# One PSUM tile for each bank in place of four tiles of two banks, in a kernel of attention and two expert layers

## The chip, the cores and the metric

The kernel runs on one core of one Trainium2 chip. The metric is device time in microseconds (us): three runs of the kernel before took 1152.51, 1151.09 and 1156.83 us, with a median of 1152.51 us. Lower is better.

## The reference

Four sequences with eight heads of 576 positions and 64 features go through a causal attention with a decay, and the 2304 rows that come out of it go through two layers of 512 by 2048 by 512.

```python
def _attn_ref(q, k, v, f):
    scores = scale * np.matmul(q, k.transpose(0, 1, 3, 2))
    log_f = np.log(np.clip(f, 0.0001, 1.0))
    cum = np.cumsum(log_f, axis=-1)
    decay = cum[:, :, :, None] - cum[:, :, None, :]
    scores = np.where(causal, -1000000000.0, scores + decay)
    scores = scores - np.max(scores, axis=-1, keepdims=True)
    attn = np.exp(scores)
    attn = attn / (np.sum(attn, axis=-1, keepdims=True) + 1e-09)
    return np.matmul(attn, v)

def _moe_ref(x, w_in, w_out, alpha):
    h = x @ w_in
    g = np.maximum(h, 0.0) + alpha * np.minimum(h, 0.0)
    return g @ w_out

def _moe2_ref(x, w_in, w_out):
    h = x @ w_in
    sp = np.where(h > 20.0, h, np.log1p(np.exp(np.minimum(h, 20.0))))
    return (h * np.tanh(sp)) @ w_out
```

## The kernel before, in words

**Attention** (`stage_T`, `stage_M`, `stage_S`, `stage_R`, `stage_V`) handles two heads at a time, 16 pairs in all. `stage_M` finds the row maxima from a first product of queries and keys (L610, L612), which VectorE reduces (L620). `stage_S` computes the scores in four pieces, 288 columns of each head in two of them and 512 in the other two (L658), and ScalarE takes the exponential of both heads of a piece in one instruction (L666). GpSimd masks the diagonal blocks (L674) and adds up (L689). `stage_R` sums over the keys with a product with ones (L701), takes the reciprocal by a logarithm and an exponential on ScalarE (L706, L707) and refines it on VectorE (L708, L710). `stage_V` multiplies by the values (L731) and writes the result to X (L737).

**The layers** work on six blocks of 384 rows. Each operand is split in a high and a low part, so that a product takes three matmuls: L775, L776 and L777 for the first matrix, L840, L841 and L842 for the second one of layer one, L851, L852 and L853 for the second one of layer two. The first four of the sixteen column groups of layer one are done apart (`group_a`), the first three blocks of that while attention still runs. `prelu` (L794, L796, L800, L803) and `mish` (L820 to L832) lie between the two matrices. `mish` takes the exponential e of h on ScalarE (L820), works on it with VectorE and ScalarE, writes an intermediate u into PSUM bank 3 (L826) and reads it back (L828). L830 reads h once more and L832 multiplies on GpSimd; the split for the second matrix is L322 on ScalarE and L332 on VectorE.

**PSUM** has eight banks of 512 columns. They are allocated as four tiles of two banks, and the names of single banks are views of these tiles:

```python
banks2 = [psum.tile([P, 2, 512], F32, tag=f"b{n}", name=f"b{n}") for n in range(4)]
banks = {n: banks2[n // 2][:, n % 2] for n in range(8)}
```

In attention the pairs 0-1, 2-3 and 4-5 are handed out as wholes, one bank for each head. Bank 6 belongs to `stage_V` and bank 7 to `group_a`. In the layers banks 4 to 7 take h in turn (`bH`), and banks 0 to 3 hold the sums of the second matrix (`bA`). Layer two has only three sums (banks 0, 1 and 2, each 128 rows by 512 columns); u is in bank 3.

**What sets the order.** Every operation is put in a plan with its engine, an estimated cost, the keys that it reads and writes, and a due time. `Plan.emit` makes a list schedule of them, ten passes long, and issues the instructions in the order of the best pass. The keys name single banks. The waits themselves are set afterwards by the tile layer from the tiles that an instruction touches, in the order of issue. An engine works on its instructions in that order.

Of the kernel before, what the change touches and what calls it, by code (L numbers as in the profile page):

```python
# [237 lines left out]
def fox_attention__then__moe_prelu__then__moe_mish(  # L238
# [52 lines left out]
    psum = pool("psum", space=PSUM)  # L291
    banks2 = [psum.tile([P, 2, 512], F32, tag=f"b{n}", name=f"b{n}") for n in range(4)]
    banks = {n: banks2[n // 2][:, n % 2] for n in range(8)}

# [170 lines left out]
    SK = NQ * P  # L465
    plan.share("two", banks2[:3])
    plan.share("one", [banks[6]])
# [51 lines left out]
    def prologue():  # L519

        V, G = nc.vector, nc.gpsimd
        pk = [("P", 1, s) for s in range(len(PIECES))]
        plan.stage("pro2")
# [37 lines left out]
    def load_bias(pr, at):  # L561
        plan.stage("LB2")
        i = pr % 2
        for e in range(2):
            h = 2 * pr + e
            src = (lambda h=h: bias[h:h + 1]) if pr == 0 else (lambda h=h: biasd[h:h + 1])
            dma(at, lambda e=e, src=src: nc.sync.dma_start(BK[i][e * HALF:e * HALF + 3, :S].bitcast(F32), src().rearrange("h t n -> (h t) n") if pr else src()),
                7, r=(["bh", "bl", "bias1"] + [("P", 1, s) for s in range(len(PIECES))] if pr == 0 else ["biasd"]) + [("BK", i)],
                w=[("BKr", i, e)], issue=0.62)
# [21 lines left out]
    def stage_M(pr, at):  # L591
# [4 lines left out]
        for c in [NQ - 1, 0] + list(range(NQ - 2, 0, -1)):  # L596
# [5 lines left out]
            for n, (a, z) in enumerate(pieces):  # L602
# [25 lines left out]
        def tr():  # L628
            for c in range(NQ):
                q0 = rows(c)[0]  # L630
                half = int(q0 >= W0)
                nc.tensor.transpose(ps()[:, half, q0 - half * W0:q0 - half * W0 + P], M5[i][:, c], ident)
        plan.add("PE", 0.11 * NQ, at + 6, tr, ["ident"] + [("M5", i, c) for c in range(NQ)], [bk, ("BQ", i, 0), ("BQ", i, 1)], mode="t")
        for half, (a, z) in enumerate(((0, W0), (W0, S))):
            def fn(e, half=half, a=a, z=z):
                if e == "ACT":
                    nc.scalar.activation(BQ[i][:, a:z], ps()[:, half, :z - a], AF.Identity, bias=bvec)
                else:
                    nc.vector.tensor_scalar(BQ[i][:, a:z], ps()[:, half, :z - a], bvec, None, op0=ALU.add)
            plan.add({"ACT": c_act(z - a, True, 1), "DVE": c_dve(z - a)}, 0.0, at + 6.5, fn, [bk, "bvec"], [("BQ", i, half)])  # L640

    def stage_S(pr, at):

        i = pr % 2
        for s, piece in enumerate(PIECES):
# [4 lines left out]
            def mm(ps=ps, piece=piece):  # L650
                x = 0
                for j, a, z in piece:
# [3 lines left out]
                    for m, (l_, r_) in enumerate(passes):  # L656
                        for e in range(2):
                            nc.tensor.matmul(ps()[:, e, x:x + z - a], l_[hs[e]], r_[hs[e]], start=m == 0, stop=m == len(passes) - 1)  # L658
                    x += z - a
                if pr == 0:  # L660
# [3 lines left out]
                     [(x, i, j) for x in ("hi", "lo") for j in range(2)] + [("BQ", i, x) for x in halves]  # L664
                     + [("BKr", i, e) for e in range(2)] + [("BK", i), ("kpad", i)], [bk, ("P", i, s)], mode="k")
# [15 lines left out]
    def stage_R(pr, at):  # L681
# [8 lines left out]
        for n, j in enumerate((1, 4, 2, 3)):  # L690
            w = 2 * (S - j * P)
            plan.add({"POOL": c_pool(w, 2.25), "DVE": c_dve(w)}, 0.0, at + 0.8 * n, lambda e, j=j, w=w: add(j, e, w),
                     [("P", i, 2 if j in (1, 4) else 3)] + [("P", i, 0), ("P", i, 1)] * (j == 1), ["acc"], port=BOTH)
        ps, bk = plan.use("two")
        h2 = S // 2

        def mm():
            for half, a, z in ((0, 0, P), (0, P, h2), (1, h2, S)):
                for e in range(2):
                    src = pt_at(i, e, 0, a, z) if z == P else acc_t[:, e, a - P:z - P]  # L700
                    nc.tensor.matmul(ps()[hs[e], half, a - half * h2:z - half * h2], ones, src, start=True, stop=True)  # L701
        plan.add("PE", 4 * S / 2.4e3 + 0.02, at + 4, mm, ["acc", "ones", ("P", i, 0)], [bk, "rr", "uu"], mode="c")
        sv = lambda: ps()[:, :, :h2]
        v2 = lambda t: t.rearrange("p (a n) -> p a n", a=2)
# [5 lines left out]
        plan.add("DVE", c_dve(S), at + 6, lambda: V.scalar_tensor_tensor(  # L710
            out=uu, in0=uu, scalar=2.0, in1=rr, op0=ALU.subtract, op1=ALU.mult), ["uu", "rr"], ["uu"], port=BOTH)

    def stage_V(pr, at):
# [3 lines left out]
        for n, (a0, z) in enumerate(WIN):  # L717
# [15 lines left out]
            rk = [("P", i, s) for s, p in enumerate(PIECES) if any(y > a0 and x < z for _, x, y in p)]  # L733
            plan.add("PE", 4 * sum((y - x) / 2.4 + 2 for _, x, y in mm) / 1e3, at + n, run,
# [296 lines left out]
```

## Time and profile before

| | |
|---|---|
| median of three runs | 1152.51 us |
| profiled execution | 1155.68 us, of which the span is 1154.0 us |
| mean granted TensorE clock | 0.975 of full speed |
| TensorE matmuls, busy | 1062.2 us, 6332 instructions |
| TensorE weight loads, busy | 922.8 us |
| VectorE, ScalarE, GpSimd, busy | 775.4, 513.8 and 421.4 us |

In the profile PE is TensorE with its matmuls and PEld its weight loads, one for each matmul of the layers; both are counted busy for themselves, since a load overlaps the matmul ahead of it. DVE is VectorE, ACT ScalarE, POOL GpSimd. Attention takes the first 310 us, and the first three blocks of `group_a` are woven into it. Then come the other three blocks of `group_a` (to some 450 us), the rest of layer one with the conversion of the weights of layer two beside it (to some 693 us, where the first exponential of `mish` starts), and layer two.

### The profile page before, as it was taken

The page shows a single profiled execution, that of the slowest core. Times are in us where ns is not written, and L with a number is a line of the kernel's source. Part 1 is how long each engine was busy: PE and PEld are TensorE (multiplying, and loading weights), DVE is VectorE, ACT ScalarE, POOL GpSimd, SP SyncE. Part 2 cuts the span into 40 slices and gives each one's busy share as a digit, 9 for nine tenths or more (in the row PEclk, how much of TensorE's full clock was granted, in tenths as well). Part 3 has the DMA queues.
Part 4 walks back from the last instruction along what each step waited for, and adds up shares of the span by engine and source line. Part 5 has one row for each costly group of instructions (what it writes and reads, how often), then busy time and mean ns, then how long its engine had stood idle before and what let it go on. Part 6 is the DMA issues. An engine that isn't in the chain of part 4 may idle for free.

```text
span 1154.0 us, 17414 instructions
## 1 busy us (share of the span) xinstructions
PE 1062.2 (92%) x6332; PEld 922.8 (80%) x6332; DVE 775.4 (67%) x1670; ACT 513.8 (45%) x1021; POOL 421.4 (37%) x416
## 2 busy tenths in 40 slices
PE   7899899898979989999999999989989989999998
PEld 6666677776768889899999998768777778778896
DVE  7677866755376776778621368678867777786785
ACT  3455444444345543434332355444444444454443
POOL 2554554544345462323233242232232322323222
PEclk9878999999989999999999999999999999999999
DMA  5232212100033344545500133000000000000000
GB/s 173 79 92 84 79 35 63 53 23 22 19 119 101 110 128 154 181 153 189 164 1 1 46 110 92 10 0 28 1 10 19 1 28 1 1 28 1 28 1 28
DMA packets 55207, 70.86 MB, mean 61 GB/s; under 512 B 6576, under 2 KB 32176, under 8 KB 55120
## 3 DMA queue, kind: packets, MB, share of 16 engines
q1 hardware_dynamic: 55120, 69.75, 19.5%
q8 instruction: 49, 0.80, 0.3%
q14 instruction: 38, 0.31, 0.1%
HBM read 56.39 MB, written 13.33 MB: 60 GB/s over the span
## 4 chain that ended last, share of the span: by engine, by line
PE 69%; DVE 16%; ACT 5%; issue 5%; DMA 3%; POOL 1%; SPq 1%; DVEq 0%; POOLq 0%; ACTq 0%
PE b L775 11%; PE b L777 9%; PE b L776 9%; PE b L851 6%; PE b L853 5%; PE b L852 5%; PE b L840 5%; PE b L658 4%; PE b L842 4%; PE b L841 4%; PE b L731 4%; DVE b L826 3%; DVE junk L620 2%; DVE x L828 1%; DMA raw<-in_moe_w_in_dram 1%
## 5 line engine op out<-in xcount | busy, mean ns | idle before, releaser
L775 PE MATMUL b<-xh,w 128*128 128x384 f32 x768 | 269.6, 351 | 42.3 <-DVE x L830 10.4
L777 PE MATMUL b<-xl,w 128*128 128x384 f32 x768 | 260.2, 339 | 1.0 <-DVE xl L332 1.0
L776 PE MATMUL b<-xh,w 128*128 128x384 f32 x768 | 259.8, 338 | 0.0
L832 POOL TENSOR_TENSOR x<-x 128x384 f32<-128x384 f32 x96 | 112.8, 1175 | 310.3 <-DVE x L830 192.8
L775 PEld LDWEIGHTS b<-xh,w 128*128 128x128 f32 x768 | 145.9, 190 | 72.9 <-DVE x L830 14.5
L776 PEld LDWEIGHTS b<-xh,w 128*128 128x128 f32 x768 | 146.2, 190 | 3.2
L777 PEld LDWEIGHTS b<-xl,w 128*128 128x128 f32 x768 | 145.9, 190 | 1.5 <-DVE xl L332 1.5
L322 ACT CAST g<-x 128x384 fp32r<-128x384 f32 x120 | 61.4, 512 | 181.6 <-POOL x L832 157.0
L840 PE MATMUL b<-g,w 128*128 128x384 f32 x384 | 134.2, 349 | 8.2 <-DVE x L803 4.2
L332 POOL TENSOR_TENSOR g<-X,g 128x384 fp32r<-128x384 f32 x72 | 77.7, 1083 | 165.2 <-ACT g L322 118.1
L842 PE MATMUL b<-g,w 128*128 128x384 f32 x384 | 130.7, 340 | 0.6 <-DVE g L332 0.6
L851 PE MATMUL b<-w,g 128*128 128x512 f32 x288 | 117.1, 407 | 15.1 <-DVE b L826 10.2
L841 PE MATMUL b<-g,w 128*128 128x384 f32 x384 | 130.6, 340 | 0.0
L853 PE MATMUL b<-w,g 128*128 128x512 f32 x288 | 113.5, 394 | 0.7 <-DVE g L332 0.7
L852 PE MATMUL b<-w,g 128*128 128x512 f32 x288 | 113.3, 394 | 0.0
L800 DVE SCALAR_TENSOR_TENSOR X<-X,alph,b 128x384 f32<-128x384 f32 x72 | 43.7, 611 | 84.1 <-ACT X L794 74.0
L826 DVE SCALAR_TENSOR_TENSOR b<-x 128x384 f32<-128x384 f32 x96 | 66.9, 697 | 46.1 <-PE b L853 36.5
L620 DVE CUSTOM_DVE_ANT_0 junk<-b,tri 128x320 f32<-128x320 f32 (+3 forms) x160 | 69.2, 433 | 26.6 <-PE b L612 19.0
L840 PEld LDWEIGHTS b<-g,w 128*128 128x128 f32 x384 | 73.8, 192 | 15.5 <-DVE x L803 5.5
L851 PEld LDWEIGHTS b<-w,g 128*128 128x128 f32 x288 | 54.0, 188 | 37.6 <-DVE b L826 21.4
L794 ACT ACTIVATE X<-b 128x384 f32<-128x384 f32 x72 | 34.9, 490 | 104.1 <-PE b L777 89.9
L332 POOL TENSOR_TENSOR w<-wb,w 128x512 fp32r<-128x512 f32 x32 | 47.5, 1485 | 91.6 <-ACT w L322 91.6
(94 smaller groups left out, 2010.8 us busy)
## 6 DMA issues: line engine op xcount, KB each, us to landing
raw<-in_moe_w_in_dram SPq DMA_DIRECT2D x64, 256.0 KB
raw<-in_moe_w_out_dram SPq DMA_DIRECT2D x64, 256.0 KB
wd<-wb SPq DMA_DIRECT2D x32, 256.0 KB
raw<-wd SPq DMA_DIRECT2D x32, 256.0 KB
qkr<-in_q_dram SPq DMA_DIRECT2D x16, 288.0 KB
qkr<-in_k_dram SPq DMA_DIRECT2D x16, 288.0 KB
out_dram<-x SPq DMA_DIRECT2D x18, 256.0 KB
vt<-in_v_dram SPq DMA_DIRECT2D x16, 256.0 KB
```

The lines of the kernel that those rows point to most:

```text
L332: plan.add(engs, 0.0, at, lambda e: (nc.gpsimd if e == "POOL" else nc.vector).tensor_tensor(out=out(), in0=in0(), in1=in1(), op=ALU.subtra ...
L775: nc.tensor.matmul(ps[:, :NB], w[:, 0, c], xh[c], start=(c == 0), stop=False)
L776: nc.tensor.matmul(ps[:, :NB], w[:, 1, c], xh[c], start=False, stop=False)
L777: nc.tensor.matmul(ps[:, :NB], w[:, 0, c], xl[c], start=False, stop=(c == KC - 1))
L826: add("DVE", c_dve(NB), lambda e, m: V.scalar_tensor_tensor(out=u, in0=m, scalar=2.0, in1=e, op0=ALU.add, op1=ALU.mult), [mk, ek], [uk], BOTH)
L832: add("POOL", c_pool(NB, 2.2), lambda e, m: nc.gpsimd.tensor_tensor(out=m, in0=e, in1=m, op=ALU.mult), [ek, mk], [mk])
L840: nc.tensor.matmul(ps[:, :NB], w[:, 0, c], g[:, 0], start=first, stop=False)
L841: nc.tensor.matmul(ps[:, :NB], w[:, 1, c], g[:, 0], start=False, stop=False)
L842: nc.tensor.matmul(ps[:, :NB], w[:, 0, c], g[:, 1], start=False, stop=last)
L851: nc.tensor.matmul(ps, g[:, 0, sl], w[:, 0], start=first, stop=False)
L852: nc.tensor.matmul(ps, g[:, 0, sl], w[:, 1], start=False, stop=False)
L853: nc.tensor.matmul(ps, g[:, 1, sl], w[:, 0], start=False, stop=last)
```

## The change

Each of the eight banks becomes a tile. The pairs of attention are pairs of tiles. An instruction cannot read two tiles as one operand, so what read both banks of a pair at once becomes two instructions: the 64 exponentials of `stage_S` become 128, the 16 logarithms of `stage_R` 32, and the 16 products of the sum with its reciprocal (L708) 32. The keys of the probabilities become one for each head. The layers' code is the same but for the tiles that it writes into. The core of the diff (left out: the same change of index or key in the prologue, in the bias loads, in the transposes of `stage_M` and in `stage_V`):

```diff
-    banks2 = [psum.tile([P, 2, 512], F32, tag=f"b{n}", name=f"b{n}") for n in range(4)]
-    banks = {n: banks2[n // 2][:, n % 2] for n in range(8)}
+    banks = {n: psum.tile([P, 512], F32, tag=f"b{n}", name=f"b{n}") for n in range(8)}
...
-    plan.share("two", banks2[:3])
+    plan.share("two", [(banks[2 * n], banks[2 * n + 1]) for n in range(3)])
...
-                            nc.tensor.matmul(ps()[:, e, x:x + z - a], l_[hs[e]], r_[hs[e]], start=m == 0, stop=m == len(passes) - 1)
+                            nc.tensor.matmul(ps()[e][:, x:x + z - a], l_[hs[e]], r_[hs[e]], start=m == 0, stop=m == len(passes) - 1)
...
-            plan.add("ACT", c_act(2 * pw[s]), ai, lambda ps=ps, s=s: nc.scalar.activation(
-                Pt[i][:, :, poff[s]:poff[s] + pw[s]], ps()[:, :, :pw[s]], AF.Exp, scale=-ISC), [bk], [("P", i, s)])
+            pk = [("P", i, s, e) for e in range(2)]
+            for e in range(2):
+                plan.add("ACT", c_act(pw[s]), ai, lambda ps=ps, s=s, e=e: nc.scalar.activation(
+                    Pt[i][:, e, poff[s]:poff[s] + pw[s]], ps()[e][:, :pw[s]], AF.Exp, scale=-ISC), [bk], [pk[e]])
...
-                    plan.add("POOL", 0.0016 * 2 * w + 0.1, ai + 0.5, sel, [], [("P", i, s)])
+                    plan.add("POOL", 0.0016 * 2 * w + 0.1, ai + 0.5, sel, [], pk)
+
+    def p_keys(i, ss):
+        return [("P", i, s, e) for s in ss for e in range(2)]
...
-        plan.add("ACT", c_act(S, True, 1), at + 5, lambda: nc.scalar.activation(v2(rr), sv(), AF.Ln, bias=eps), [bk, "ones"], ["rr"])
-        plan.add("ACT", c_act(S, False), at + 5, lambda: nc.scalar.activation(rr, rr, AF.Exp, scale=-1.0), ["rr"], ["rr"])
-        plan.add("DVE", c_dve(S), at + 5.5, lambda: V.scalar_tensor_tensor(
-            out=v2(uu), in0=sv(), scalar=1e-9, in1=v2(rr), op0=ALU.add, op1=ALU.mult), [bk, "rr"], ["uu"])
+        hh2 = [slice(x * h2, (x + 1) * h2) for x in range(2)]
+        for x in range(2):
+            plan.add("ACT", c_act(h2, True, 1), at + 5, lambda x=x: nc.scalar.activation(rr[:, hh2[x]], ps()[x][:, :h2], AF.Ln, bias=eps),
+                     [bk, "ones"], [("rr", x)])
+        rk = [("rr", x) for x in range(2)]
+        plan.add("ACT", c_act(S, False), at + 5, lambda: nc.scalar.activation(rr, rr, AF.Exp, scale=-1.0), rk, rk)
+        for x in range(2):
+            plan.add("DVE", c_dve(h2), at + 5.5, lambda x=x: V.scalar_tensor_tensor(
+                out=uu[:, hh2[x]], in0=ps()[x][:, :h2], scalar=1e-9, in1=rr[:, hh2[x]], op0=ALU.add, op1=ALU.mult), [bk] + rk, ["uu"])
```

The order of instructions is shown below with the semaphores that an instruction waits for. A PSUM tile is named b0 to b3 before (each two banks) and b0 to b7 after (one bank each); the number behind it is a running one. Lines after the change are seven higher in the layers' code, but for the helper of the split, where L332 becomes L331.

TensorE in layer two before, about 855 us into the span: the second matrix for the last two column groups of a block (L851 to L853), with its sums in the tiles b0 (banks 0 and 1) and b1 (bank 2, beside u in bank 3).

```order
L851 MATMUL b1_66<-w14_1_6185,g2_102 128x512
L852 MATMUL b1_66<-w14_1_6185,g2_102 128x512
L853 MATMUL b1_66<-w14_1_6185,g2_102 128x512
L851 MATMUL b0_65<-w15_1_6187,g3_103 128x512 [waits Activation_49]
L852 MATMUL b0_65<-w15_1_6187,g3_103 128x512
L853 MATMUL b0_65<-w15_1_6187,g3_103 128x512 [waits DVE_49]
L851 MATMUL b1_66<-w15_1_6187,g3_103 128x512 [waits DVE_49]
L852 MATMUL b1_66<-w15_1_6187,g3_103 128x512
L853 MATMUL b1_66<-w15_1_6187,g3_103 128x512
```

The same place after the change; bank 2 is now the tile b2.

```order
L858 MATMUL b2_67<-w14_1_6285,g2_106 128x512
L859 MATMUL b2_67<-w14_1_6285,g2_106 128x512
L860 MATMUL b2_67<-w14_1_6285,g2_106 128x512
L858 MATMUL b0_65<-w15_1_6287,g3_107 128x512 [waits Activation_49]
L859 MATMUL b0_65<-w15_1_6287,g3_107 128x512
L860 MATMUL b0_65<-w15_1_6287,g3_107 128x512 [waits DVE_49]
L858 MATMUL b2_67<-w15_1_6287,g3_107 128x512
L859 MATMUL b2_67<-w15_1_6287,g3_107 128x512
L860 MATMUL b2_67<-w15_1_6287,g3_107 128x512
```

The matmuls stand in the same order. The wait of the last group of three for VectorE is no longer there; the two waits for its operand g3 are.

VectorE at the same place before: L826 writes u into bank 3 (tile b1), L828 reads it, L830 reads h (tile b2).

```order
L826 SCALAR_TENSOR_TENSOR b1_66<-x2_2_113 128x384 [waits PE_49,Activation_49]
L830 SCALAR_TENSOR_TENSOR x2_2_113<-x2_2_113,b2_67 128x384 [waits DVE_49]
L828 SCALAR_TENSOR_TENSOR x2_2_113<-b1_66,x2_2_113 128x384 [waits PE_49]
L826 SCALAR_TENSOR_TENSOR b1_66<-x2_2_113 128x384 [waits DVE_49,Activation_49]
L830 SCALAR_TENSOR_TENSOR x2_2_113<-x2_2_113,b2_67 128x384 [waits DVE_49]
L828 SCALAR_TENSOR_TENSOR x2_2_113<-b1_66,x2_2_113 128x384
L332 TENSOR_TENSOR g0_100<-x2_2_113,g0_100 128x384 [waits Activation_49]
```

The same place after; u is in the tile b3, h in b4 and b5.

```order
L833 SCALAR_TENSOR_TENSOR b3_68<-x2_2_117 128x384 [waits Activation_49]
L837 SCALAR_TENSOR_TENSOR x2_2_117<-x2_2_117,b4_69 128x384 [waits DVE_49]
L835 SCALAR_TENSOR_TENSOR x2_2_117<-b3_68,x2_2_117 128x384
L833 SCALAR_TENSOR_TENSOR b3_68<-x2_2_117 128x384 [waits DVE_49,Activation_49]
L837 SCALAR_TENSOR_TENSOR x2_2_117<-x2_2_117,b5_70 128x384 [waits DVE_49]
L835 SCALAR_TENSOR_TENSOR x2_2_117<-b3_68,x2_2_117 128x384
L331 TENSOR_TENSOR g0_104<-x2_2_117,g0_104 128x384 [waits PE_49,Activation_49]
```

The waits of L826 and L828 for TensorE are gone, and the split into g0 now names TensorE itself: it waits for the last matmul that read that buffer.

ScalarE in attention before: the four exponentials of one pair of heads, each of two banks.

```order
L666 ACTIVATE Pt1_119<-b0_65 128x2x512 [waits PE_49]
L666 ACTIVATE Pt1_119<-b1_66 128x2x288 [waits PE_49]
L666 ACTIVATE Pt1_119<-b0_65 128x2x288 [waits PE_49]
L666 ACTIVATE Pt1_119<-b1_66 128x2x512 [waits PE_49]
L322 CAST khl1_125<-qkr1_121 128x576 [waits DMAHW3_49]
```

ScalarE in attention after, where most of the exponentials of one pair stand; wb0, xh3, khl1 and qhl1 belong to other work.

```order
L667 ACTIVATE Pt1_123<-b0_65 128x512 [waits PE_49,Pool_49]
L667 ACTIVATE Pt1_123<-b1_66 128x512 [waits PE_49]
L399 ACTIVATE wb0_92<-raw0_91 128x256 [waits DMAHW7_49,Pool_49]
L399 ACTIVATE wb0_92<-raw0_91 128x256 [waits DMAHW0_49]
L321 CAST xh3_99<-X_111 128x384 [waits DVE_49]
L667 ACTIVATE Pt1_123<-b2_67 128x288 [waits PE_49]
L667 ACTIVATE Pt1_123<-b3_68 128x288 [waits PE_49]
L667 ACTIVATE Pt1_123<-b0_65 128x512 [waits DVE_49,PE_49]
L321 CAST khl1_129<-qkr1_125 128x576 [waits DMAHW3_49]
L321 CAST qhl1_127<-qkr1_125 128x576 [waits DMAHW4_49]
L667 ACTIVATE Pt1_123<-b1_66 128x512 [waits DVE_49,PE_49]
```

There are twice as many exponentials of half the size, each with a wait of its own, and the plan has laid other work between them. In attention and in layer one the order of all engines differs from before in many places; in layer two it is the same on every engine.

## Rows read from the trace of the kernel before

**Rows 1.** The page's first part: busy us, share of the span, instructions.
```profile
PE 1062.2 (92%) x6332; PEld 922.8 (80%) x6332; DVE 775.4 (67%) x1670; ACT 513.8 (45%) x1021; POOL 421.4 (37%) x416
```

**Rows 2.** Table by stage: window, its length, busy us of each engine, clock, DMA.
```profile
40.00:310.00 270.00, 245.43 (x2064) 185.21 (x2065) 173.83 (x497) 123.85 (x206) 132.23 (x153) 0.92 0.18 53
310.00:450.00 140.00, 122.47 (x648) 115.21 (x647) 100.27 (x223) 67.10 (x155) 67.73 (x54) 0.96 0.35 111
450.00:570.00 120.00, 113.95 (x631) 111.66 (x630) 89.30 (x195) 48.34 (x115) 34.44 (x32) 0.97 0.57 181
570.00:693.00 123.00, 121.97 (x699) 120.59 (x697) 43.05 (x63) 44.17 (x91) 42.25 (x40) 1.00 0.16 44
693.00:1140.00 447.00, 417.29 (x2014) 356.91 (x2015) 337.78 (x596) 212.35 (x425) 129.73 (x110) 1.00 0.05 16
```

**Rows 3.** Timeline at 855 us: start, duration, engine, line; idle before and releaser.
```profile
853.24 0.19 PEld L775 LDWEIGHTS b<-xh,w 128*128 128x128 f32 x1
...
854.81 0.19 PEld L851 LDWEIGHTS b<-w,g 128*128 128x128 f32 x1
...
855.91 0.19 PEld L853 LDWEIGHTS b<-w,g 128*128 128x128 f32 x1
...
856.61 0.19 PEld L853 LDWEIGHTS b<-w,g 128*128 128x128 f32 x1
856.64 0.57 DVE L826 SCALAR_TENSOR_TENSOR b<-x 128x384 f32<-128x384 f32 x1 [1.42 <-PE b L853]
...
857.26 0.19 PEld L851 LDWEIGHTS b<-w,g 128*128 128x128 f32 x1 [0.47 <-DVE b L826]
```

**Rows 4.** Weight loads from 693 to 1140 us by line: count, busy, mean ns, idle before.
```profile
L775 PEld LDWEIGHTS b<-xh,w 128*128 128x128 f32 x379 | 71.1, 188 | 31.9 <-DVE x L830 14.5 <-ACT x L820 10.1 <-issue 4.0
L852 PEld LDWEIGHTS b<-w,g 128*128 128x128 f32 x278 | 52.2, 188 | 6.6
L851 PEld LDWEIGHTS b<-w,g 128*128 128x128 f32 x278 | 52.1, 188 | 35.5 <-DVE b L826 21.4 <-DVE x L828 4.4 <-issue 1.3
...
L840 PEld LDWEIGHTS b<-g,w 128*128 128x128 f32 x15 | 2.8, 187 | 1.1 <-DVE x L828 0.7 <-DVE x L894 0.4
```

**Rows 5.** Waits of weight loads, 693 to 1140 us: total us, times, longest us.
```profile
PEld b L851 <- DVE b L826: 21.4, 26, 1.4
PEld b L775 <- DVE x L830: 14.5, 17, 2.5
PEld b L775 <- ACT x L820: 10.1, 14, 1.0
```

**Rows 6.** VectorE's waits from 693 to 1140 us: total us, times, longest us.
```profile
DVE b L826 <- PE b L853: 33.1, 28, 2.0
DVE x L828 <- PE b L853: 21.4, 30, 1.6
DVE x L821 <- ACT x L820: 17.9, 19, 1.8
DVE g L332 <- ACT g L322: 11.8, 31, 0.6
DVE b L826 <- ACT x L825: 7.8, 16, 1.5
```

**Rows 7.** Weight loads of L775, from 310 to 450 us: as in group 4.
```profile
L775 PEld LDWEIGHTS b<-xh,w 128*128 128x128 f32 x115 | 21.7, 188 | 18.3 <-DVE X L800 8.3 <-ACT x L322 2.8 <-ACT x L794 1.8
```

**Rows 8.** Weight loads of L775, from 450 to 693 us: as in group 4.
```profile
L775 PEld LDWEIGHTS b<-xh,w 128*128 128x128 f32 x221 | 42.1, 191 | 10.0 <-DVE X L800 5.5 <-ACT X L794 4.3
```

**Rows 9.** Waits of weight loads in attention, from 0 to 310 us.
```profile
PEld b L775 <- DVE X L737: 6.6, 6, 2.1
```

**Rows 10.** Attention's ScalarE instructions by shape: count, busy, mean ns, idle before.
```profile
L666 ACT ACTIVATE Pt<-b 128x1024 f32<-128x1024 f32 x32 | 32.7, 1025 | 25.7 <-PE b L658 24.6 <-DVE uu L708 0.9
L666 ACT ACTIVATE Pt<-b 128x576 f32<-128x576 f32 x32 | 20.7, 649 | 17.6 <-PE b L658 15.2 <-issue 2.3
```

**Rows 11.** A stretch of attention with a low clock, columns as in group 2.
```profile
80.00:100.00 20.00, 18.16 (x124) 11.21 (x124) 15.52 (x51) 6.42 (x11) 8.30 (x10) 0.66 0.24 62
```

More of the change, by code (lines that the diff above doesn't have):

```diff
@@ L521, in prologue @@
         V, G = nc.vector, nc.gpsimd
-        pk = [("P", 1, s) for s in range(len(PIECES))]
+        pk = [("P", 1, s, e) for s in range(len(PIECES)) for e in range(2)]
         plan.stage("pro2")
@@ L567, in load_bias @@
             dma(at, lambda e=e, src=src: nc.sync.dma_start(BK[i][e * HALF:e * HALF + 3, :S].bitcast(F32), src().rearrange("h t n -> (h t) n") if pr else src()),
-                7, r=(["bh", "bl", "bias1"] + [("P", 1, s) for s in range(len(PIECES))] if pr == 0 else ["biasd"]) + [("BK", i)],
+                7, r=(["bh", "bl", "bias1"] + [("P", 1, s, e) for s in range(len(PIECES)) for e in range(2)] if pr == 0 else ["biasd"]) + [("BK", i)],
                 w=[("BKr", i, e)], issue=0.62)
@@ L609, in mm @@
                     for e in range(2):
-                        nc.tensor.matmul(ps()[:, e, :z - a], qhl[i][hs[e], 0, q0:q0 + P], khl[i][hs[e], 0, a:z], start=True, stop=False)
+                        nc.tensor.matmul(ps()[e][:, :z - a], qhl[i][hs[e], 0, q0:q0 + P], khl[i][hs[e], 0, a:z], start=True, stop=False)
                     for e in range(2):
-                        nc.tensor.matmul(ps()[:, e, :z - a], BQ1[hs[e]], BK[i][hs[e], a:z], start=False, stop=True)
+                        nc.tensor.matmul(ps()[e][:, :z - a], BQ1[hs[e]], BK[i][hs[e], a:z], start=False, stop=True)
                     if pr == 0:
@@ L620, in stage_M @@
                              nc.vector.tensor_tensor_reduce(
-                                 out=junk[ql, :z - a], in0=ps()[ql, e, :z - a], in1=tri[ql, x0 + a:x0 + z],
+                                 out=junk[ql, :z - a], in0=ps()[e][ql, :z - a], in1=tri[ql, x0 + a:x0 + z],
                                  scale=-1.0, scalar=BIG if n == 0 else nmx[ql, e:e + 1], op0=ALU.add, op1=ALU.min,
@@ L631, in tr @@
                 half = int(q0 >= W0)
-                nc.tensor.transpose(ps()[:, half, q0 - half * W0:q0 - half * W0 + P], M5[i][:, c], ident)
+                nc.tensor.transpose(ps()[half][:, q0 - half * W0:q0 - half * W0 + P], M5[i][:, c], ident)
         plan.add("PE", 0.11 * NQ, at + 6, tr, ["ident"] + [("M5", i, c) for c in range(NQ)], [bk, ("BQ", i, 0), ("BQ", i, 1)], mode="t")
@@ L636, in fn @@
                 if e == "ACT":
-                    nc.scalar.activation(BQ[i][:, a:z], ps()[:, half, :z - a], AF.Identity, bias=bvec)
+                    nc.scalar.activation(BQ[i][:, a:z], ps()[half][:, :z - a], AF.Identity, bias=bvec)
                 else:
-                    nc.vector.tensor_scalar(BQ[i][:, a:z], ps()[:, half, :z - a], bvec, None, op0=ALU.add)
+                    nc.vector.tensor_scalar(BQ[i][:, a:z], ps()[half][:, :z - a], bvec, None, op0=ALU.add)
             plan.add({"ACT": c_act(z - a, True, 1), "DVE": c_dve(z - a)}, 0.0, at + 6.5, fn, [bk, "bvec"], [("BQ", i, half)])
@@ L664, in stage_S @@
                      [(x, i, j) for x in ("hi", "lo") for j in range(2)] + [("BQ", i, x) for x in halves]
-                     + [("BKr", i, e) for e in range(2)] + [("BK", i), ("kpad", i)], [bk, ("P", i, s)], mode="k")
-            plan.add("ACT", c_act(2 * pw[s]), ai, lambda ps=ps, s=s: nc.scalar.activation(
-                Pt[i][:, :, poff[s]:poff[s] + pw[s]], ps()[:, :, :pw[s]], AF.Exp, scale=-ISC), [bk], [("P", i, s)])
+                     + [("BKr", i, e) for e in range(2)] + [("BK", i), ("kpad", i)], [bk] + [("P", i, s, e) for e in range(2)], mode="k")
+            pk = [("P", i, s, e) for e in range(2)]
+            for e in range(2):
+                plan.add("ACT", c_act(pw[s]), ai, lambda ps=ps, s=s, e=e: nc.scalar.activation(
+                    Pt[i][:, e, poff[s]:poff[s] + pw[s]], ps()[e][:, :pw[s]], AF.Exp, scale=-ISC), [bk], [pk[e]])
             for j, a, z in piece:
@@ L692, in stage_R @@
             plan.add({"POOL": c_pool(w, 2.25), "DVE": c_dve(w)}, 0.0, at + 0.8 * n, lambda e, j=j, w=w: add(j, e, w),
-                     [("P", i, 2 if j in (1, 4) else 3)] + [("P", i, 0), ("P", i, 1)] * (j == 1), ["acc"], port=BOTH)
+                     p_keys(i, [2 if j in (1, 4) else 3] + [0, 1] * (j == 1)), ["acc"], port=BOTH)
         ps, bk = plan.use("two")
@@ L700, in mm @@
                     src = pt_at(i, e, 0, a, z) if z == P else acc_t[:, e, a - P:z - P]
[L701 to L704, printed above, removed]
+                    nc.tensor.matmul(ps()[half][hs[e], a - half * h2:z - half * h2], ones, src, start=True, stop=True)
+        plan.add("PE", 4 * S / 2.4e3 + 0.02, at + 4, mm, ["acc", "ones"] + p_keys(i, [0]), [bk, "uu"] + [("rr", x) for x in range(2)], mode="c")
         V = nc.vector
-        plan.add("ACT", c_act(S, True, 1), at + 5, lambda: nc.scalar.activation(v2(rr), sv(), AF.Ln, bias=eps), [bk, "ones"], ["rr"])
-        plan.add("ACT", c_act(S, False), at + 5, lambda: nc.scalar.activation(rr, rr, AF.Exp, scale=-1.0), ["rr"], ["rr"])
-        plan.add("DVE", c_dve(S), at + 5.5, lambda: V.scalar_tensor_tensor(
-            out=v2(uu), in0=sv(), scalar=1e-9, in1=v2(rr), op0=ALU.add, op1=ALU.mult), [bk, "rr"], ["uu"])
+        hh2 = [slice(x * h2, (x + 1) * h2) for x in range(2)]
[7 more added lines that the diff above has]
+                out=uu[:, hh2[x]], in0=ps()[x][:, :h2], scalar=1e-9, in1=rr[:, hh2[x]], op0=ALU.add, op1=ALU.mult), [bk] + rk, ["uu"])
         plan.add("DVE", c_dve(S), at + 6, lambda: V.scalar_tensor_tensor(
-            out=uu, in0=uu, scalar=2.0, in1=rr, op0=ALU.subtract, op1=ALU.mult), ["uu", "rr"], ["uu"], port=BOTH)
+            out=uu, in0=uu, scalar=2.0, in1=rr, op0=ALU.subtract, op1=ALU.mult), ["uu"] + rk, ["uu"], port=BOTH)
     def stage_V(pr, at):
@@ L732, in run @@
                                          start=m == 0, stop=m == len(mm) - 1)
-            rk = [("P", i, s) for s, p in enumerate(PIECES) if any(y > a0 and x < z for _, x, y in p)]
+            rk = p_keys(i, [s for s, p in enumerate(PIECES) if any(y > a0 and x < z for _, x, y in p)])
             plan.add("PE", 4 * sum((y - x) / 2.4 + 2 for _, x, y in mm) / 1e3, at + n, run,
```

## Prediction, made before the result was known

> **What bounds the kernel now.** I read the page first, then the table by stage, then what the weight loads of TensorE waited for. On the page TensorE's matmuls are busy for 92% of the span, and no other engine reaches 70% [rows 1]. So TensorE's own order sets the time, and a gain must come from holes in it. The table shows where these can be. From 570 to 693 us matmuls follow each other with no hole (122.0 of 123 us busy, 699 in 123 us); from 310 to 450 us and in layer two, from 693 to 1140 us, they don't [rows 2].
>
> How much is lost there I take from the spacing of weight loads, of which there is one for each matmul. In an undisturbed piece of layer two the nine loads of 384-column matmuls that start from 853.24 us on take until 854.81, 0.174 us for each, and those of 512 columns take 0.70 us for three, from 855.91 to 856.61, which is 0.233 us [rows 3]. Layer two between 693 and 1140 us has 2015 loads [rows 2]; three times 379 are of the first matrix, three times 15 left over from layer one, and some 833 of the second matrix [rows 4]. That makes 1182 x 0.174 + 833 x 0.233 = 399.8 us of work in 447 us: 47.2 us are lost.
>
> The Trainium skill, in "Trainium Kernel Development and Optimization", section "Performance Expectations", says that matmul busy time is a bad measure of the distance from the bound and that the busy share of weight loads is a good one. By the matmuls' busy time only 447 - 417.3 = 29.7 us could be had in this stage [rows 2]; by the loads it is 47.2. The rows agree with the skill: a load stands idle for 0.47 us at 857.26 while the matmul before it is still counted busy.
>
> Now the cause. At 856.64 us VectorE's L826 writes u into bank 3, and it had waited 1.42 us for a matmul L853. Then the weight load of L851 at 857.26, for a sum in bank 2, waits 0.47 us for L826 [rows 3]. Neither reads what the other writes: they share a tile, b1, and nothing else. Over the stage this one pair of lines costs TensorE 21.4 us in 26 stalls, and VectorE 33.1 us the other way round [rows 5, 6]. The same is seen between L775 and the readers of h in the other bank of its tile: it waits 10.1 us for the exponential L820, though a bank is free again only when L830, later, has read it, so that such a wait cannot be for its own bank [rows 5].
>
> **The change part by part.** In layer two nothing moves: all engines keep their order. What changes is the waits. In the order before, 31 matmuls L851 wait for L826, 27 for L828 and 37 matmuls L775 for L820; after, none do. L775's waits for L830 grow from 51 to 91: they now name the last reader of its own bank, four column groups back, which is long done.
>
> *Layer two.* Away go L851's stalls for L826 and L828, 21.4 + 4.4 us, less the 0.045 us (0.233 - 0.188) that a load of this kind is idle anyway, in 33 stalls: 24.3 us. Away go the 10.1 us for L820. Of the 14.5 us for L830 I take four fifths, 11.6, since the rows don't say which bank each stall was for [rows 4, 5]. That is 46.0 us, nearly all that is lost. What is late next is the split for the second matrix, L322 and L332. To be in time VectorE must keep up: it is busy 337.8 us of the 447, and its waits for ScalarE (17.9 + 11.8 + 7.8) bring that to 375, while the waits for TensorE, 54.5 us, go [rows 2, 6]. A stage of 405 us leaves it 30 us. I take 42 us back of the 46; the ends are 15 (below) and all of the 47.2.
>
> *Layer one.* From 310 to 450 us L775 waits 18.3 us, mostly for `prelu` (L800, L794) on the neighbouring bank [rows 7]; from 450 to 693 us it waits 10.0 [rows 8]. VectorE is busy 72% and 74% of the time up to 570 us [rows 2], and converts weights whose order the plan has changed. I take 13 and 7 us back; the ends are 0 and all 28.3.
>
> *Attention.* Bank 6 (`stage_V`) and bank 7 (`group_a`) shared a tile: L775 waits 6.6 us for L737 [rows 9]. I take half of it back, 3 us. Against it stand more and smaller instructions. An exponential of 1024 columns takes 1025 ns, one of 576 takes 649, so a column costs 0.84 ns and an instruction 166 ns apart from its columns [rows 10]. 64 more of them are 10.6 us, and the 16 more logarithms and 16 more products on VectorE some 5 us at the same price. ScalarE is busy 124 of 270 us here, so its share lies beside TensorE's 245 us [rows 2]. On the path of a pair there can be at most one more exponential, one logarithm and one product, 3 x 0.166 x 16 = 8 us if nothing covers them. TensorE has the next pair's scores and `group_a` to do meanwhile, so I take 3 us. Without that cover it is the 8. The new order itself I bound by +-10 us, about one stall of 0.6 us in each pair, and take 0, for both plans have the same matmuls between the first and the last of attention.
>
> The Trainium skill, in "Perfetto Trace Analysis", section "Optimizing Scalar/DVE Operations", speaks against this part: it gives about 51 ns of access overhead for each ScalarE instruction on PSUM, about twice that as profiled, and advises larger operations where the engine is saturated. By its 102 ns the 64 exponentials would cost some 6.5 us, an estimate, and by the rows 10.6; the engine is not saturated here, so neither enters the sum.
>
> *Sum.* 42 + 13 + 7 + 3 - 3 = 62 us. The profiled execution took 1155.7 us, 3.2 above the median of 1152.5; from it the sum gives 1093.7, and on the scale of the median 1090.5. I predict 1090 us.
>
> **The rivals.** *VectorE becomes the pace of layer two.* Its idle time there is 447 - 337.8 = 109 us, of which the 54.5 for TensorE go. If the rest stays, it needs 392.5 us, just under TensorE's 399.8. For: both are close, it works in order, and a chain of `mish` crosses it six times. Against: its waits for ScalarE are in part a result of TensorE's stalls. If half of the 54.5 us return as waits for ScalarE or GpSimd, the stage takes 420 us and gives 27 instead of 42; with 5 and 3 in layer one the sum is 35 and the time 1117 us. In the worst form that I allow, 15 us of layer two alone less 8 in attention, it is 1145.
>
> *Nothing is gained: the waits are only renamed.* Then a stalled L775 or L851 finds its own operand late by the same amount, and the time is 1152. For: each has other waits left (for the split, for L830). Against: the largest releasers of the loads are all neighbours in a tile, none is the split, and with TensorE's stalls the split's own start was late as well [rows 4, 5].
>
> *Slower through attention's clock.* From 80 to 100 us the granted clock is 0.66 of full speed, between the two levels of 1.2 and 2.4 GHz, and over 40 to 310 us it is 0.92 [rows 2, 11]. More single waits in attention could keep TensorE at the lower level for longer. If all of the stage had 0.66, its 245.4 us of matmuls would grow by 245.4 x (0.92 / 0.66 - 1) = 97 us, and the time would be 1187. The mechanism decides from the point where it eats the 62 us, a mean clock of 0.735. For: the plan interleaves otherwise. Against: after 100 us the filling matmuls of `group_a` are there as before, so it would have to lose in all of the first 100 us and more.
>
> **How the numbers follow.** The forecast has 0.80, the VectorE rival 0.13, no gain 0.04, the clock 0.03. The lower end: all of 47.2 + 28.3 + 6.6 would give 1070, and a better order in attention 6 more: 1064. The upper end takes in the VectorE rival's 1117 and some more of its way to 1145: 1126. What a measurement of this kernel can tell from no change is about 0.5%, or 6 us. Forecast and VectorE rival are faster, together 0.93; of the no-gain case three quarters are the same, 0.03; the rest and the clock are slower, 0.04.
>
> **What would show it.** Weight loads of L851's counterpart should no longer be released by L826's, nor VectorE's by TensorE there; layer two should shrink from 447 us to about 405 with loads 0.174 and 0.233 us apart. Idle time ahead of L775 from 310 to 450 us should fall from 18.3 us to under 6. The exponentials should take some 0.41 and 0.60 us. If the loads of the second matrix now wait for L322 or L332, the VectorE rival is right; if attention ends later than at 310 us by more than 10 us, the cost there was misjudged. The prediction is wrong if the time is over 1126 us.

## The result, and the profile after

The changed kernel takes 1066.4 us (median of four runs, 1062.31 to 1069.25), the one before beside it on the same chip 1154.38. The ratio is 0.9237 with a 95% interval of 0.9196 to 0.9278. The forecast was 1090 us, within 1064 to 1126: the direction and the cause hold, the gain is 88 us instead of 62, and the time lies only 2 us above the lower end of the range.

The first part of the page after the change, to be held against [rows 1]:

```profile
PE 1023.7 (97%) x6332; PEld 922.4 (87%) x6332; DVE 770.8 (73%) x1686; ACT 520.0 (49%) x1101; POOL 421.8 (40%) x416
```

No engine got less to do: ScalarE has 80 instructions more and VectorE 16. In the shorter span every engine's share went up, that of the weight loads from 80% to 87%. As many matmuls are counted busy for 38.5 us less.

The table by stage after the change, with the columns of [rows 2]; the windows are set to the same stages, which now begin earlier:

```profile
40.00:300.00 260.00, 243.40 (x2099) 187.65 (x2100) 180.53 (x529) 134.09 (x295) 136.17 (x157) 0.95 0.20 59
300.00:420.00 120.00, 111.10 (x615) 108.83 (x614) 100.97 (x215) 63.16 (x145) 65.22 (x51) 0.97 0.42 128
420.00:540.00 120.00, 119.23 (x688) 118.94 (x688) 88.48 (x200) 51.45 (x120) 38.05 (x35) 1.00 0.58 185
540.00:650.00 110.00, 110.00 (x637) 110.00 (x636) 37.13 (x56) 40.87 (x85) 39.00 (x37) 1.00 0.15 42
650.00:1048.00 398.00, 398.00 (x2016) 362.04 (x2015) 336.43 (x599) 212.27 (x425) 129.37 (x112) 1.00 0.05 18
```

Layer two does the 2015 weight loads that took 447 us in 398.0, and TensorE's matmuls are counted busy there without a hole. VectorE does the same 336 us of work in that shorter time, 85% of it. From 420 us on matmuls follow each other as densely as they did before only from 570 us on.

The weight loads of layer two by line, and all that is left of their waits for another engine ([rows 4, 5] before; L782 is the L775 of before, L858 the L851):

```profile
L782 PEld LDWEIGHTS b<-xh,w 128*128 128x128 f32 x380 | 71.4, 188 | 4.5 <-DVE x L837 0.5
...
L858 PEld LDWEIGHTS b<-w,g 128*128 128x128 f32 x277 | 52.0, 188 | 7.9
L859 PEld LDWEIGHTS b<-w,g 128*128 128x128 f32 x276 | 51.8, 188 | 7.9
```

```profile
PEld b L782 <- DVE x L837: 0.5, 2, 0.3
```

The first line of a group of three is now idle as long as the second, 7.9 us, and its row names no releaser: what is left is the spacing of the matmuls, which the second line showed before as well (6.6 us [rows 4]). 31.9 and 35.5 us of idle time became 4.5 and 7.9. VectorE's own waits in this stage, to be held against [rows 6]:

```profile
DVE x L828 <- ACT x L827: 16.3, 22, 1.4
DVE g L331 <- ACT g L321: 15.4, 38, 1.0
DVE xl L331 <- ACT xh L321: 11.2, 3, 4.4
DVE b L833 <- ACT x L832: 10.3, 24, 2.0
...
DVE x L323 <- PE b L860: 0.2, 1, 0.2
```

The waits for TensorE are gone, and those for ScalarE have grown: these four lines make 53 us where the three of [rows 6] make 37.5, and the growth lies in the two lines of the split (L331). With 336 us of work and 53 us of waits for ScalarE, VectorE has only some 8 of the 398 us left, but TensorE does not notice.

In layer one, from 300 to 420 us, L782 waits 3.2 us instead of the 18.3 of [rows 7]:

```profile
L847 PEld LDWEIGHTS b<-g,w 128*128 128x128 f32 x101 | 19.9, 197 | 7.9 <-DVE x L810 7.8
...
L782 PEld LDWEIGHTS b<-xh,w 128*128 128x128 f32 x104 | 19.5, 188 | 3.2 <-DVE X L807 1.5 <-ACT x L321 1.2 <-DVE x L323 0.5
```

From 420 to 650 us, where [rows 8] has 10.0 us, it waits for nothing:

```profile
L782 PEld LDWEIGHTS b<-xh,w 128*128 128x128 f32 x220 | 41.3, 188 | 0.0
```

What is left in this stage is the wait of the second matrix for `prelu`, which was there before (310 to 450 us, L840 is L847 and L803 is L810):

```profile
L840 PEld LDWEIGHTS b<-g,w 128*128 128x128 f32 x101 | 20.2, 200 | 5.6 <-DVE x L803 4.6 <-DVE x L324 1.0
```

L810 writes no operand of L847. It reads h from PSUM, so with one tile for each bank this is a wait for the bank itself, which h leaves and a sum of the second matrix takes.

The split exponentials, to be held against [rows 10]:

```profile
L667 ACT ACTIVATE Pt<-b 128x512 f32<-128x512 f32 x64 | 34.9, 597 | 22.3 <-PE b L657 22.1
L667 ACT ACTIVATE Pt<-b 128x288 f32<-128x288 f32 x64 | 22.6, 413 | 20.4 <-PE b L657 19.4 <-issue 0.9
```

One takes 597 or 413 ns, as the slope had it. 64 of each at these means would be 64.6 us, but ScalarE is busy with them for 57.5 us, which is 4.1 us more than the 53.4 of before. Neighbours overlap in the profile: two that follow each other take 0.71 and 1.09 us together, where one of double size took 0.649 and 1.025 [rows 10].

```profile
72.58 0.71 ACT L667 ACTIVATE Pt<-b 128x288 f32<-128x288 f32 x2 [0.63 <-PE b L657]
75.27 1.09 ACT L667 ACTIVATE Pt<-b 128x512 f32<-128x512 f32 x2 [1.98 <-PE b L657]
```

### The profile page after: what moved, and what is told of

Read it like the earlier page. It is cut to its first block, busy times and chain, and to the rows that moved or that the text cites. A ratio compares the mean times of both kernels' runs of the same rounds, so it can differ in the third digit from the quotient of the medians.

```text
span 1060.5 us, 17610 instructions
## 1 busy us (share of the span) xinstructions
PE 1023.7 (97%) x6332; PEld 922.4 (87%) x6332; DVE 770.8 (73%) x1686; ACT 520.0 (49%) x1101; POOL 421.8 (40%) x416
## 4 chain that ended last, share of the span: by engine, by line
PE 81%; DVE 9%; DMA 4%; issue 3%; ACT 1%; SPq 0%; POOL 0%; DVEq 0%; ACTq 0%
PE b L782 11%; PE b L784 11%; PE b L783 11%; PE b L859 6%; PE b L858 6%; PE b L860 6%; PE b L657 5%; PE b L847 5%; PE b L738 5%; PE b L849 4%; PE b L848 4%; DVE junk L619 2%; PE b L609 2%; DVE wb L405 2%; DVE wb L403 2%
## 5 line engine op out<-in xcount | busy, mean ns | idle before, releaser
L782 PE MATMUL b<-xh,w 128*128 128x384 f32 x768 | 260.5, 339 | 3.5 <-DVE x L807 1.3
L783 PE MATMUL b<-xh,w 128*128 128x384 f32 x768 | 257.4, 335 | 0.0
L782 PEld LDWEIGHTS b<-xh,w 128*128 128x128 f32 x768 | 144.1, 188 | 13.5 <-issue 2.2
L783 PEld LDWEIGHTS b<-xh,w 128*128 128x128 f32 x768 | 144.2, 188 | 3.9
L847 PE MATMUL b<-g,w 128*128 128x384 f32 x384 | 132.6, 345 | 8.0 <-DVE x L810 7.2
L331 POOL TENSOR_TENSOR g<-X,g 128x384 fp32r<-128x384 f32 x72 | 78.2, 1090 | 155.3 <-ACT g L321 124.2
L860 PE MATMUL b<-w,g 128*128 128x512 f32 x288 | 113.1, 393 | 0.0
L859 PE MATMUL b<-w,g 128*128 128x512 f32 x288 | 113.1, 393 | 0.0
L858 PE MATMUL b<-w,g 128*128 128x512 f32 x288 | 113.0, 392 | 0.0
L331 DVE TENSOR_TENSOR g<-x,g 128x384 fp32r<-128x384 f32 x102 | 75.5, 742 | 16.9 <-ACT g L321 16.7
L399 ACT ACTIVATE wb<-raw 128x256 f32<-128x256 f32 x128 | 52.5, 433 | 69.0 <-DMA wd<-wb 33.8
L847 PEld LDWEIGHTS b<-g,w 128*128 128x128 f32 x384 | 73.1, 190 | 12.5 <-DVE x L810 8.4
L667 ACT ACTIVATE Pt<-b 128x512 f32<-128x512 f32 (+1 forms) x128 | 57.1, 505 | 42.8 <-PE b L657 41.5
L401 DVE TENSOR_SCALAR wb<-wb 128x256 int32<-128x256 int32 x128 | 54.5, 443 | 31.6 <-ACT wb L399 30.9
```

The lines of the kernel that those rows point to most:

```text
L331: plan.add(engs, 0.0, at, lambda e: (nc.gpsimd if e == "POOL" else nc.vector).tensor_tensor(out=out(), in0=in0(), in1=in1(), op=ALU.subtra ...
L782: nc.tensor.matmul(ps[:, :NB], w[:, 0, c], xh[c], start=(c == 0), stop=False)
L783: nc.tensor.matmul(ps[:, :NB], w[:, 1, c], xh[c], start=False, stop=False)
L847: nc.tensor.matmul(ps[:, :NB], w[:, 0, c], g[:, 0], start=first, stop=False)
L858: nc.tensor.matmul(ps, g[:, 0, sl], w[:, 0], start=first, stop=False)
L859: nc.tensor.matmul(ps, g[:, 0, sl], w[:, 1], start=False, stop=False)
```

## The experiments

The change has three parts: the tiles, the instructions that have to be split, and the order that the plan makes of the split operations. The first three kernels separate them. For this an operation of the plan can issue two instructions, so that cost, key and place in the order stay as before; with tiles all joined, such a kernel has the same order as the one before on all engines. Each kernel was timed beside the kernel before, on the same chip. A ratio goes with that neighbour's time, so ratios and not times are to be held against each other.

| kernel | tiles | instructions | order | time, us | ratio to before, 95% interval |
|---|---|---|---|---|---|
| before | 4 of two banks | joint | old | 1154.4 beside the changed kernel, 1152.5 beside e1 to e4, 1155.3 beside e5 to e7 | 1 |
| changed | 8 of one bank | split | new | 1066.4 | 0.9237 [0.9196, 0.9278] |
| e1 | 8 of one bank | split | old | 1067.7 | 0.927 [0.9244, 0.9296] |
| e2 | 4 of two banks | split | new | 1160.1 | 1.0079 [1.0049, 1.0109] |
| e3 | 4 of two banks | split | old | 1156.0 | 1.0019 [0.999, 1.0049] |
| e4 | 2 and 3 single | split there | old | 1113.7 | 0.9662 [0.9641, 0.9683] |
| e5 | 4 to 7 single | split there | old | 1098.9 | 0.952 [0.9467, 0.9572] |
| e6 | 6 and 7 single | joint | old | 1123.1 | 0.9727 [0.9685, 0.9769] |
| e7 | all single but 0 and 1 | split but there | old | 1069.4 | 0.9262 [0.9218, 0.9307] |

To see where a gain lies I cut each profiled execution at two marks, the start of attention's last write to X (L737) and of the first exponential of `mish` (L820). Length of the three pieces in us, in which the woven-in work makes the first mark a little soft. Each row is a single execution, up to 4 us off the median of its kernel (before 3.2 above, changed 4.1 below), so differences of a few us between rows say nothing:

| kernel | to the last write of X | to the first exponential of `mish` | layer two, to the end |
|---|---|---|---|
| before | 310.4 | 382.7 | 460.9 |
| changed | 293.9 | 356.7 | 409.9 |
| e1 | 291.0 | 361.7 | 409.9 |
| e2 | 317.9 | 377.7 | 462.8 |
| e3 | 311.7 | 379.6 | 461.0 |
| e4 | 310.8 | 378.3 | 424.4 |
| e5 | 289.8 | 361.6 | 444.4 |
| e6 | 292.0 | 373.2 | 455.9 |
| e7 | 292.1 | 365.3 | 413.1 |

**e1: the tiles, in the old order.**

```diff
-    banks2 = [psum.tile([P, 2, 512], F32, tag=f"b{n}", name=f"b{n}") for n in range(4)]
-    banks = {n: banks2[n // 2][:, n % 2] for n in range(8)}
+    SPLIT = (0, 1, 2, 3)
+    banks2 = {n: psum.tile([P, 2, 512], F32, tag=f"b{n}", name=f"b{n}") for n in range(4) if n not in SPLIT}
+    banks = {n: psum.tile([P, 512], F32, tag=f"s{n}", name=f"s{n}") if n // 2 in SPLIT else banks2[n // 2][:, n % 2]
+             for n in range(8)}
+
+    def both(pair, wide):
+        # one operand of both banks where they are one tile, else one of each
+        return [(slice(0, 2), wide)] if wide is not None else [(e, pair[e]) for e in range(2)]
...
-            plan.add("ACT", c_act(2 * pw[s]), ai, lambda ps=ps, s=s: nc.scalar.activation(
-                Pt[i][:, :, poff[s]:poff[s] + pw[s]], ps()[:, :, :pw[s]], AF.Exp, scale=-ISC), [bk], [("P", i, s)])
+            plan.add("ACT", c_act(2 * pw[s]), ai, lambda ps=ps, s=s: [nc.scalar.activation(
+                Pt[i][:, e, poff[s]:poff[s] + pw[s]], x[..., :pw[s]], AF.Exp, scale=-ISC) for e, x in both(ps()[0], ps()[1])], [bk], [("P", i, s)])
...
```

> All eight banks are tiles of their own and the split instructions are there, but in the order of the kernel before: each operation of the plan keeps its cost and key, and issues two instructions where it has to. Theory 1 (waits between neighbours in a tile are the loss): 75 to 90 of the 88 us that the change gave, a time of 1065 to 1080 us, with attention ending near 294 us as after the change. Theory 2 (a part of the gain, the 16 us in attention above all, is the plan's new order): some 20 us less, 1085 to 1095 us, with attention ending near 310 us as before.

1067.7 us, and attention ends at 291.0 us. Theory 1 is right: the tiles give all of it in the old order, and the new order is worth nothing that can be told apart (0.927 and 0.9237, with intervals that overlap).

**e2: the split instructions and the new order, on the old tiles.**

```diff
-    banks = {n: psum.tile([P, 512], F32, tag=f"b{n}", name=f"b{n}") for n in range(8)}
+    banks2 = [psum.tile([P, 2, 512], F32, tag=f"b{n}", name=f"b{n}") for n in range(4)]
+    banks = {n: banks2[n // 2][:, n % 2] for n in range(8)}
```

> The order, the keys and the split instructions of the changed kernel, but the banks are views of four tiles of two banks as before. Theory 1: all is lost again, 1150 to 1160 us. Theory 2: attention keeps its 16 us and layer one some of its 26, 1125 to 1135 us.

1160.1 us: everything is lost again, and 0.5 to 1.1% more. The edit is to the changed kernel, whose order stays the same on every engine, and with the tiles joined the waits of layer two come back to within 0.2 us ([rows 5]; L859 is L851, L783 is L775, L834 is L826):

```profile
PEld b L859 <- DVE b L834: 21.4, 26, 1.4
PEld b L783 <- DVE x L838: 14.4, 16, 2.5
PEld b L783 <- ACT x L828: 10.3, 14, 1.1
```

**e3: the split instructions alone.** As e1, but the four tiles of two banks stay and each joint operation is issued as two.

```diff
...
-            plan.add("ACT", c_act(2 * pw[s]), ai, lambda ps=ps, s=s: nc.scalar.activation(
-                Pt[i][:, :, poff[s]:poff[s] + pw[s]], ps()[:, :, :pw[s]], AF.Exp, scale=-ISC), [bk], [("P", i, s)])
+            plan.add("ACT", c_act(2 * pw[s]), ai, lambda ps=ps, s=s: [nc.scalar.activation(
+                Pt[i][:, e, poff[s]:poff[s] + pw[s]], x[..., :pw[s]], AF.Exp, scale=-ISC) for e, x in both(ps()[0], None)], [bk], [("P", i, s)])
...
```

> The kernel before, with its tiles and its order; only the 64 exponentials, 16 logarithms and 16 products are issued as two instructions each. This is the cost of the edit's visible part by itself. My sum put 3 us on it and at most 8: 1152 to 1162 us. If more instructions in themselves help (the next engine starts earlier on a half), under 1150.

1156.0 us, a ratio of 1.0019 whose interval goes from 1 us of gain to 6 us of loss. It holds the 3 us of my sum and also nothing; the 8 us that I allowed at most are outside.

**e4: only banks 2 and 3 apart.** e1's code with banks 0-1, 4-5 and 6-7 as tiles of two.

```diff
-    SPLIT = (0, 1, 2, 3)
+    SPLIT = (1,)
```

> Order of the kernel before; only banks 2 and 3 are tiles of their own, so only the intermediate u of the second layer no longer shares a tile with a sum (in attention this pair of banks takes split instructions). By the trace of before the stalls of this pair are 25.8 us of TensorE's. Theory 1: 22 to 30 us faster than before, 1122 to 1132 us, with the rest of the stalls (those for the readers of h) as they were. Rival: the stalls for u hide those for h, so that one without the other gives under 12 us, 1140 to 1150.

1113.7 us, 39 us faster: more than the stalls of these banks, and both theories are off in size. Layer two alone is 36.5 us shorter, where the pair's own stalls were 25.8. The waits of its weight loads show where the rest is from (L781 is L775, L826 the exponential that was L820, L836 the L830):

```profile
PEld b L781 <- ACT x L826: 9.2, 13, 1.0
PEld b L781 <- DVE x L836: 4.3, 6, 1.0
PEld b L857 <- ACT x L831: 1.3, 1, 1.3
```

The tiles of h were not touched, yet L775's wait for VectorE's L830 fell from 14.5 us [rows 5] to 4.3. These 10.2 us and the 25.8 make 36.0 of the 36.5. L830 stands in VectorE's queue with L826 and L828, which had waited 33.1 and 21.4 us for matmuls that write bank 2 [rows 6]; in e4 neither waits for TensorE any more. So the loss of a shared tile went round, it seems: TensorE held up VectorE's write of u, this held up its reading of h, and this TensorE at another tile. That L830 came late by just this way is read from the queue's order; no run isolates it.

**e5: only banks 4 to 7 apart.** `SPLIT = (2, 3)`.

> Order of the kernel before; banks 4 to 7 are tiles of their own, banks 0 to 3 stay two tiles. So h takes turns over four tiles in both layers, and the bank of the products with the values no longer shares with that of the woven-in layer work; u still shares with a sum. If the two parts add (all tiles alone gave 85 us in this order, banks 2 and 3 gave 39), 46 us are left for this one: 1104 to 1110 us, with attention ending near 293 us and layer two taking some 444 us, from the first exponential on. Rival: a stall that goes lets the one for u grow, so the parts overlap: 25 to 35 us, 1117 to 1128, layer two over 452 us.

1098.9 us, a ratio of 0.952, which is 55 us of 1152.5 and above the 46 expected. Layer two takes 444.4 us, as expected if the parts add; 16.5 here and 36.5 in e4 make 53.0 against the 51.0 of both. Up to the first exponential of `mish` this kernel wins 41.7 us, as much as e1 does with all tiles (40.4). So nearly all of the gain ahead of layer two is from banks 4 to 7. The parts overlap by some 5 us there (4.0 in e4) and by 2 in layer two.

**e6: only banks 6 and 7 apart.** `SPLIT = (3,)`; no instruction is split.

> Order of the kernel before; only banks 6 and 7 are tiles of their own. This asks where attention's 16 to 19 us come from. Theory A (products with the values and the woven-in layer work held each other up): attention ends at 291 to 296 us, and one of the two h pairs is free, which gives some 15 us more in the layers: 1118 to 1126 us. Theory B (attention's gain comes from the pairs of banks 0 to 5, where one head's bank no longer waits for the other's): attention ends at 306 us or later, 1130 to 1140 us.

1123.1 us, with the last write of X at 292.0 us: theory A. The kernel before shows how the two banks held each other up. Here the product with the values in bank 6 (L731, eight matmuls) is done at 190.65 us:

```profile
189.78 0.87 PE L731 MATMUL b<-Pt,vt 128*64 128x256 f32 x8 [0.18 <-ACT x L794]
...
191.89 0.34 PE L777 MATMUL b<-xl,w 128*128 128x384 f32 x1
...
192.27 0.42 DVE L737 SCALAR_TENSOR_TENSOR X<-b,uu 128x256 f32<-128x256 f32 x1 [0.47 <-PE b L777]
...
192.75 0.44 PE L775 MATMUL b<-xh,w 128*128 128x384 f32 x1 [0.52 <-DVE X L737]
```

VectorE's L737, which reads bank 6, waits 0.47 us for L777 of `group_a` in bank 7, and then the next L775 in bank 7 waits 0.52 us for L737. Three lines of waits up to 310 us (L322 copies a sum out of bank 7) stand beside the 6.6 us of [rows 9]; all four lie between a user of bank 6 and one of bank 7, and e6 has none of them:

```profile
PEld b L840 <- DVE X L737: 2.3, 3, 0.9
DVE x L796 <- PE b L731: 4.8, 3, 2.2
ACT x L322 <- PE b L731: 7.9, 3, 3.5
```

The longest waits of L737 look like the same thing, but most of them is a wait for its own matmuls:

```profile
295.19 2.28 PE L731 MATMUL b<-Pt,vt 128*64 128x320 f32 x20
...
298.93 0.49 DVE L737 SCALAR_TENSOR_TENSOR X<-b,uu 128x320 f32<-128x320 f32 x1 [8.00 <-PE b L842]
```

L731 ends at 297.47 us, so no more than 1.46 of the 8.00 us are due to bank 7. In e6 (L743 is L737, L737 is L731) the last write to X still waits for its own product:

```profile
292.01 0.49 DVE L743 SCALAR_TENSOR_TENSOR X<-s,uu 128x320 f32<-128x320 f32 x1 [3.34 <-PE s L737]
```

The stage in e6, cut at 292 us, with the columns of [rows 2]:

```profile
40.00:292.00 252.00, 236.44 (x2084) 179.96 (x2083) 176.07 (x505) 124.88 (x209) 135.75 (x156) 0.96 0.20 59
```

Some 20 matmuls more than in [rows 2] are done in 18 us less. TensorE's idle time falls from 24.6 to 15.6 us, and its matmuls are busy for 236 us instead of 245 at a mean granted clock of 0.96 instead of 0.92. How much the clock does is better seen from e3 and e1, which differ in nothing but the tiles:

```profile
40.00:312.00 272.00, 244.85 (x2074) 184.52 (x2072) 175.50 (x522) 130.76 (x285) 134.66 (x156) 0.94 0.19 55
40.00:291.00 251.00, 239.48 (x2063) 182.44 (x2063) 175.51 (x515) 128.90 (x281) 133.59 (x153) 0.95 0.20 57
```

Attention's mark moves by 20.7 us between them. The idle time falls by 15.6 us (27.2 to 11.5), while the clock goes from 0.94 to 0.95, which by these rows is worth about 4 us (an estimate: 0.06 of 272 us less 0.05 of 251). The holes are the larger part. The two later pieces of e6 are 14.5 us shorter than before, as theory A had it.

**e7: all apart but banks 0 and 1.** `SPLIT = (1, 2, 3)`.

> Order of the kernel before; all banks are tiles of their own but 0 and 1, which stay one tile, so the pieces of attention that land there keep one exponential for both heads. In the layers banks 0 and 1 hold sums that are written for a whole block and read once at its end, so sharing should cost little: 1066 to 1073 us. Rival: every pair costs as 2 and 3 did, 1080 us or more. Under 1064 us, the fewer instructions of attention are worth something and this is a better version.

1069.4 us, a ratio of 0.9262 beside e1's 0.927. Two sums that are written for a whole block and read at its end may share a tile at no cost that shows, and 28 of the 96 splits fewer in attention are no gain either. It is no better version than the changed kernel.

## Why the prediction was right, and where it was too small

**The cause** held. Weight loads waited for instructions on the neighbouring bank of their tile. e1 differs from e3, and the changed kernel from e2, in nothing but the tiles, and in either order the tiles bring the whole gain.

**The number.** The time came out 24 us under the forecast, and it is luck that the range holds it. All the holes that I had found would have given 1070 us; the last 6 us of the range, down to 1064, stand for a better order in attention, and e1 shows none that can be told from nothing. The measured 1066.4 lies in just these 6 us. Of the 93.5 us between the two profiled executions 51.0 lie in layer two, 26.0 in layer one and 16.5 in attention.

**Layer two: 42 us forecast, 49 measured** in the window up to 1140 us (51.0 to the end). The mis-sized step is "I take 42 us back of the 46". The amount lost, 47.2 us, was about right. But I held 4 us back for what would be late next, and nothing was. I also counted each stall apart; in e4 they hung together, 36.5 us for stalls of 25.8.

**Layer one: 20 us forecast, 26.0 measured.** Of the 28.3 us of L775's waits I took 20, again as a reserve for conversion work that VectorE shares. It did not come due: 3.2 us of these waits are left, and the second matrix's wait for `prelu` grew from 5.6 to 7.9 us.

**Attention: 0 forecast (3 - 3), 16.5 measured, and 18.4 by banks 6 and 7 alone in e6.** This is the term that was furthest off. "I take half of it back, 3 us" looked only at L775's 6.6 us. The same two banks also held up L840 for 2.3 us, VectorE's L796 for up to 4.8 and ScalarE's copy of a sum for up to 7.9, none of which [rows 9] holds. As in layer two, such waits seem to come back through the queues, and there are more of them than the rows price: TensorE's idle time in the stage fell by 9.0 us from the kernel before to e6, and by 15.6 from e3 to e1, and the clock did the smaller part. How the gain divides among the single waits no run tells.

**The cost of the split instructions, 3 us,** is inside what e3 allows (-1 to 6 us). The order by itself, taken as 0 with 10 us either way, cannot be told from 0 on the new tiles (0.9237 and 0.927); on the old ones e2 and e3 differ by some 0.6%, about what can be told apart.

**The rivals.** VectorE did not become the pace, but it came close, as the rival said: its 336 us of work and 53 us of waits for ScalarE make nearly 390 of the 398 us. TensorE shows no wait for the split or the exponentials there, and 0.5 us for L837. The waits were not renamed, as L858's row without a releaser shows. Attention's clock did not go down: the four profiled executions with banks 6 and 7 in one tile have 0.92 to 0.94 from 40 us to their first mark, the five with them apart 0.95 or 0.96.

**Matmul busy time against weight loads.** By the matmuls' busy time 29.7 us were to be had in layer two, by the spacing of the loads 47.2; the stage gave 49. The rule of the Trainium skill, "Trainium Kernel Development and Optimization", section "Performance Expectations", that matmul busy time is a bad measure of how close a kernel is to its bound, holds here. The loads' busy share of the stage rose from 80% to 91% (362.0 of 398 us), and there it ends, since a load is counted as 188 ns where a 512-column matmul takes 233.

## What to carry to other kernels

Where waits are set by tile, a tile is a lock: two engines that work on different banks of it wait for each other in both directions. Look in the waits for a pair of lines that have no data in common, and price both directions, since the engine that is not the bottleneck passes its wait on through its queue. A wait that names the neighbour last can still be mostly one for the engine's own data, so look when that was done. Here the whole loss came back, as the engines behind TensorE had just enough idle time for the shorter stage. Sharing between buffers that are written and read in the same rhythm, as the two sums in banks 0 and 1, cost nothing that shows (e7).

## What the runs showed that was not expected

Splitting ScalarE's instructions cost less than the durations of single ones say: 64 more at 166 ns, by the slope of [rows 10], would be 10.6 us, but the engine was busy for only 4.1 us more with them, and e3 finds no more than 6 us in the whole kernel. And with fewer holes attention's mean granted clock was higher, 0.95 (changed) and 0.96 (e6) instead of 0.92. That gives some time back a second time, but only some: the kernel before, timed 21 times beside e1 to e7, had a mean clock over the whole span of 0.967 to 0.984, a range that takes in all four executions of e6 (0.981 to 0.983).
